# Three tiles move from one float32 product to split products with accumulating transfers, under a new instruction order

## The chip, the cores and the metric

The kernel runs on one core of a Trainium2 chip. The metric is the device time of one execution in microseconds, the median of several runs.

## What is computed

Four batches of eight heads run a gated linear recurrence over 768 steps of width 48; the result, 3072 tokens of width 384, goes through a feed-forward layer of width 2048 with a gate that is a clipped ramp.

```python
f = 1.0 / (1.0 + np.exp(-f_logit))
for t in range(S):
    state = f[:, :, t, :, None] * state + np.einsum('bhd,bhe->bhde', k[:, :, t], v[:, :, t])
    y[:, :, t] = np.einsum('bhd,bhde->bhe', q[:, :, t], state)
...
h = x @ w_in
relu6 = np.clip(h + 3.0, 0.0, 6.0)
g = h * relu6 / 6.0
return (g @ w_out)
```

## The kernel before

**Units and groups.** The recurrence is cut into 24 units, each one batch and one chunk of 128 steps. Four units (one chunk of all batches) make a group of 512 tokens, and there are six groups. On a unit i the steps are: `load`, `loadq`, `loadv` (transfers that SyncE issues), `gate` (sigmoid, ScalarE), `back` and `fwd` (scans, VectorE, L428 and L448), `kmul` and `qmul` (VectorE, L441 and L454), `rend` (two short VectorE instructions, L444 and L445), then on TensorE `tk` (transposes, L516), `kv` (L537), `att` (L497), `qs` (L571) and `av` (L587), with ScalarE's `ktok` (L523) between `tk` and `kv`, VectorE's `mask` (L504) between `att` and `av`, and `xh`, `xs`, `xl` that write the group's input rows.

**The feed-forward layer.** There are 16 slices f of the width 2048. For each group and slice, `mm1` multiplies into a PSUM bank, `relu` (ScalarE) and `g` (VectorE) form the gated value, and `mm2` adds to three PSUM banks. Numbers after these names count 16 per group, so `mm2.5` is slice 5 of group 0. Values are split into a high and a low float16 part: `gh` writes the high part on ScalarE (L683), `gl` the low part as a subtraction (L693), and `mm2` then needs nine float16 products (L709). For group 0 the slices 0 to 4 are done in halves (`mm1a`, `mm1b`, `mm2a`, `mm2b`) with float32 second products (L846), and slices 5 to 7 have `mm2x` (L720), three float32 products of 512 columns straight from the gated value. Groups 2 to 5 use a recombined form of the first product (`p1` to `p8`, L772).

**Weights.** Each slice's weights arrive as raw 64-bit numbers (`ld`, L284) and are turned to numbers by `z`, `cy` (ScalarE), `mid`, `dif`, `top` (VectorE, L301, L308, L312), then split: `high` on ScalarE (L317) and `low`, or its halves `lowi` (first product) and `lowo` (second product), by subtraction (L320).

**What sets the order.** `ORDER` is one list of steps; each step appends its instructions to its engine's queue, and every engine runs its queue in that order. So the list alone decides what stands behind what on PE, DVE, ACT, POOL and SP. `ON_POOL` names steps that GpSimd does in VectorE's place. `warm.n` (L1071) puts n blocks of 128 columns of products on zeros into TensorE's queue, whose result nobody reads. `hold` makes a step of a PSUM pair wait for the last `qs` there.

**The end.** The last group is written in two full thirds (`od.15`, `od.16` with 256 KB each) and two halves (`odh`), by ScalarE's queue. `flag0`, `finite`, `count` and `judge` gather a number that decides whether a slow general path follows.

## Time and profile before

| What | Value |
|---|---|
| median of 3 runs | 456.9 us (456.84 to 457.68) |
| the profiled execution's own time | 457.2 us |
| its span, first to last instruction | 455.5 us |
| TensorE busy | 448.7 us, 99% of the span |
| VectorE, ScalarE, GpSimd busy | 358.3, 231.2, 18.7 us |

The profiled execution spends 1.7 us outside its span and is 0.3 us longer than the median. A row of the chain of waits gives the start, the length and the engine and line of a piece of the work that ended last. A row of the timeline gives start, length, engine, line, operation, tiles, shapes and count, and in brackets the idle time before it with what ended it. Neighbouring instructions of an engine overlap by some 0.05 to 0.1 us in the timeline, and matmuls' ends are modelled.

### The profile page before, as it was taken

Reading aid. Unit: us, or ns where it says so; the run is one execution under the profiler, and the core shown is the slowest. Engines: PE = TensorE matmul, PEld = TensorE weight load, DVE = VectorE, ACT = ScalarE, POOL = GpSimd, SP = SyncE. Lnnn points to the kernel's source line nnn. Section 1 sums busy time; section 2 is a strip of 40 time slices with the busy share of each in tenths; the row PEclk is TensorE's granted clock in tenths of the full one; section 3 lists DMA queues with packets and bytes.
Section 4 is the critical chain, followed back from the end, with each engine's and each line's share of the span. In section 5 each row is a group of like instructions: output and inputs, shape, how many; then the busy total and the mean of one; then the engine's idle time right before and its main releaser. Section 6 shows DMA issues by size and latency. Waiting matters only on the chain.

```text
span 455.5 us, 12559 instructions
## 1 busy us (share of the span) xinstructions
PE 448.7 (99%) x5449; PEld 291.5 (64%) x5449; DVE 358.3 (79%) x643; ACT 231.2 (51%) x389; POOL 18.7 (4%) x31
## 2 busy tenths in 40 slices
PE   8899999999999999999999999999999999999996
PEld 4578755544455556686767676666676757677764
DVE  6999999879999999989986764888583676466562
ACT  3776777765454445554454265255263444442531
POOL 3000211231000000000000000000000000000000
PEclk9999999999999999999999999999999999999999
DMA  8679556550142512204202340040000010030002
GB/s 284 221 257 388 221 192 250 204 167 4 52 130 95 164 47 76 92 3 121 89 1 85 83 150 6 22 142 2 1 10 1 5 30 2 1 115 2 1 0 73
DMA packets 25531, 43.18 MB, mean 95 GB/s; under 512 B 2560, under 2 KB 17408, under 8 KB 25472
## 3 DMA queue, kind: packets, MB, share of 16 engines
q1 hardware_dynamic: 23872, 41.56, 27.1%
q8 instruction: 43, 0.70, 0.6%
q10 hardware_dynamic: 1600, 0.79, 0.6%
q14 instruction: 16, 0.13, 0.1%
HBM read 36.43 MB, written 4.72 MB: 90 GB/s over the span
## 4 chain that ended last, share of the span: by engine, by line
PE 96%; DVE 2%; ACT 1%; issue 0%; DVEq 0%; ACTq 0%
PE o L709 35%; PE pair L772 16%; PE single L772 9%; PE pair L664 7%; PE single L664 5%; PE pair L497 3%; PE o L846 3%; PE pair L587 3%; PE pair L571 3%; PE pair L537 2%; PE idle L1071 2%; PE o L720 2%; PE pair L516 2%; PE pair L862 1%; PE o_half L862 1%; PE single L828 1%
## 5 line engine op out<-in xcount | busy, mean ns | idle before, releaser
L709 PE MATMUL o<-gg,weight 128*128 128x512 f16 x744 | 173.4, 379 | 0.0
L709 PEld LDWEIGHTS <-weight 128*128 128x128 f16 x744 | 71.7, 98 | 73.8
L772 PEld LDWEIGHTS <-weight 128*128 128x128 f16 x672 | 65.1, 98 | 13.3 <-issue 0.2
L772 PE MATMUL pair<-xmem,wide 128*128 128x256 f16 x384 | 51.2, 273 | 0.0
L683 ACT ACTIVATE gg<-raws 128x512 f16<-128x512 f32 x64 | 38.4, 624 | 23.9 <-DVE raws L806 8.1
L772 PE MATMUL single<-xmem,weight 128*128 128x256 f16 x384 | 49.8, 273 | 0.2 <-DVE raws L806 0.2
L801 ACT ACTIVATE raws<-pair,half 128x512 f32<-128x512 f32 x32 | 21.5, 684 | 42.3 <-PE pair L772 33.3
L772 PEld LDWEIGHTS <-wide 128*128 128x128 f16 x384 | 36.9, 98 | 8.7 <-DVE single L787 0.6
L801 ACT ACTIVATE raws<-single,half 128x512 f32<-128x512 f32 x32 | 22.0, 687 | 39.8 <-PE single L772 32.2
L664 PEld LDWEIGHTS <-weight 128*128 128x128 f16 x243 | 23.1, 98 | 26.7 <-issue 0.3
L772 PE MATMUL pair<-xmem,weight 128*128 128x256 f16 x288 | 36.5, 273 | 0.0
L806 DVE SCALAR_TENSOR_TENSOR raws<-raws,single 128x512 f32<-128x512 f32 x32 | 21.8, 682 | 18.3 <-ACT raws L801 18.3
L693 DVE TENSOR_TENSOR gg<-raws,gg 128x512 f16<-128x512 f32 x48 | 31.9, 683 | 5.0 <-ACT gg L683 5.0
L664 PE MATMUL pair<-xmem,weight 128*128 128x512 f16 x144 | 33.2, 379 | 0.0
L806 DVE SCALAR_TENSOR_TENSOR raws<-raws,pair 128x512 f32<-128x512 f32 x32 | 21.5, 682 | 12.3 <-ACT raws L801 12.1
L787 DVE TENSOR_TENSOR pair<-pair,raws 128x512 f32<-128x512 f32 x16 | 11.2, 697 | 25.3 <-PE pair L772 17.1
L448 DVE TENSOR_TENSOR_SCAN suffix<-gates,rend 112x516 f32<-112x516 f32 x24 | 29.6, 1235 | 0.1
L428 DVE TENSOR_TENSOR_SCAN suffix<-gates,unit 112x516 f32<-112x516 f32 x23 | 28.0, 1223 | 0.1
L664 PE MATMUL single<-xmem,weight 128*128 128x512 f16 x99 | 23.2, 380 | 0.0
L674 ACT ACTIVATE tg<-pair,half 128x512 f32<-128x512 f32 x16 | 10.9, 686 | 19.5 <-PE pair L664 16.3
L683 ACT ACTIVATE gg<-tg 128x512 f16<-128x512 f32 x24 | 14.4, 626 | 9.0 <-DVE tg L678 5.2
L504 DVE TENSOR_TENSOR a<-pair,causal 128x512 f32<-128x512 f32 x24 | 16.3, 684 | 2.3 <-PE pair L497 1.3
(133 smaller groups left out, 639.5 us busy)
## 6 DMA issues: line engine op xcount, KB each, us to landing
qkf<-qk SPq DMA_DIRECT2D x24, 512.0 KB, 4.6
raws<-w SPq DMA_DIRECT2D x16, 768.0 KB, 5.7
gates<-fg SPq DMA_DIRECT2D x23, 258.5 KB, 3.6
v<-v SPq DMA_DIRECT2D x24, 200.0 KB, 3.7
outT<-os SPq DMA_DIRECT2D x11, 256.0 KB, 3.1
outT<-os SPq DMA_DIRECT2D x8, 128.0 KB, 1.9
wide<-wide SPq DMA_DIRECT2D x32, 24.0 KB, 2.0
outT<-os ACTq DMA_DIRECT2D x2, 256.0 KB, 4.1
```

The source lines that it names most:

```text
L428: nc.vector.tensor_tensor_scan(flat(sf)[:, ::-1], gt[:, 1:][:, ::-1], flat(unit)[:, ::-1], 0.0, op0=ALU.mult, op1=ALU.add,)
L448: nc.vector.tensor_tensor_scan(flat(sf), gt[:, :NP * (C + 1)], flat(rend), 0.0, op0=ALU.mult, op1=ALU.add,)
L497: nc.tensor.matmul(d["at"][HC * odd:HC * (odd + 1), e, 2 * n + c], t[rs, 1, n, c, odd], t[rs, 0, n, c, odd], start=not growing[at], stop=T ...
L504: nc.vector.tensor_tensor(d["a"].rearrange("r p e t -> r e p t"), d["at"], causal.unsqueeze(1).unsqueeze(1).broadcast_to([128, 2, NP, HC]) ...
L571: nc.tensor.matmul(d["y"][to:to + 64, odd, n, cs], before[rs, p], t[rs, 0, n, c, odd], start=alone and (odd, e) not in seen, stop=False, s ...
L664: nc.tensor.matmul(h, win[:, f, a, k * 128:(k + 1) * 128], g["xt"][:, k, :g["n"] // C, b], start=i == 0, stop=i == 3 * KT - 1,)
L683: nc.scalar.activation(d["gg"][:, 0], d["t"], AF.Copy)
L693: engine("gl", int(g["name"]) * NF + f).tensor_tensor(d["gg"][:, 1], d["t"], d["gg"][:, 0], op=ALU.subtract)
L709: nc.tensor.matmul(g["o"][m], wout[:, f, a, m * 128:(m + 1) * 128], g[f]["gg"][:, b], start=f == 0 and i == 0, stop=f == NF - 1 and i == 2 ...
L772: nc.tensor.matmul(to[:, n * 256:(n + 1) * 256], weights(q, n, a), g["wide"][:, :, block - 3, b], start=fresh and count == 1, stop=count = ...
L801: nc.scalar.activation(to, src, AF.Relu, bias=half, scale=RISE)
L806: nc.vector.scalar_tensor_tensor(to, to, TOP, src, op0=ALU.min, op1=ALU.mult)
```

## The change

1. The slices 5, 6 and 7 of group 0 no longer use three float32 products but nine float16 products as the others do. Their low parts are made without a subtraction: ScalarE writes the negated high part (`gn` for the gated value, `lno` for the weights), and GpSimd issues a transfer that adds the float32 value to it, from SBUF to SBUF (`gl.5` to `gl.7` and `lowo.5` to `lowo.7`, in the list `ON_DMA`). There are six such transfers, three `gn`, three `lno` and three more `gh`.
2. All of `ORDER` is another permutation. The blocks of `warm` are the same ten steps with 39 blocks, at other places. One `seed` (a product on zeros ahead of `count`) is gone.
3. Ahead of each `qs` a new `apart` puts a wait into TensorE's queue for the last `att`, `kv` or `av` of the same PSUM pair.
4. Of the four last transfers, three are issued by SyncE; the last one, of the second half, stays on ScalarE.

```diff
+ON_DMA = """
+gl.5 gl.6 gl.7 lowo.5 lowo.6 lowo.7
+""".split()
 ORDER = """
-load.0 loadh.0 gate.0 gateh.0 back.0 backh.0 loadq.0 loadv.0 rend.0 kmul.0 load.1 fwd.0 gate.1 back.1 warm.16 tk.0.3
...
+warm.16 load.0 loadh.0 gate.0 warm.4 warm.1 gateh.0 back.0 backh.0 rend.0 loadq.0 loadv.0 warm.1 warm.3 warm.3 load.1
...
+    def apart(at):
+
+        if touched[at] is not None:
+            after(nc.tensor.nop().ins, touched[at], mybir.DependencyClass.Sync)
+            touched[at] = None
+
+    def touch(at):
+        touched[at] = nc.cur_bb.bb.instructions[-1]
...
+    def conv_minus(f, half):
+        nc.scalar.activation(two(weight[:, f, 1])[:, half], both(f)[:, half], AF.Copy, scale=-1.0)
+
     def conv_low(op, f, half):
+        if f"{op}.{f}" in ON_DMA:
+            nc.gpsimd.dma_start(
+                out=two(weight[:, f, 1])[:, half], in_=both(f)[:, half], accum_op=ALU.add
+            )
+            return
...
         def qs():
             t = chunks[i]
             at, half = pair()
+            apart(at)
...
+    def gneg(g, f):
+        d = g[f]
+        nc.scalar.activation(d["gg"][:, 1], d["t"], AF.Copy, scale=-1.0)
+
     def glow(g, f):
         d = g[f]
+        if f"gl.{int(g['name']) * NF + f}" in ON_DMA:
+            nc.gpsimd.dma_start(out=d["gg"][:, 1], in_=d["t"], accum_op=ALU.add)
+            return
...
-            (nc.scalar if g is groups[-1] else nc.sync).dma_start(
+            (nc.scalar if g is groups[-1] and part == 1 else nc.sync).dma_start(
```

`touch(at)` is called at the end of `att`, `kv` and `av`.

TensorE's queue, from its first products to unit 0's `kv`, before (L1071 is `warm`, L516 `tk`, L537 the first of 48 products of `kv`):

```order
L1071 MATMUL idle<-blank 128x512 x4
L516 MATMUL pair_71<-ident,qkf_137 128x112 x4
L1071 MATMUL idle<-blank 128x512
L537 MATMUL pair_70<-v_139,ktok_156 64x48
L537 MATMUL pair_70<-v_139,ktok_156 48x48
```

The same place now (L1103 is `warm`, L538 `tk`, L559 `kv`):

```order
L1103 MATMUL idle<-blank 128x512 x5
L1103 MATMUL idle<-blank 128x128 x2
L1103 MATMUL idle<-blank 128x384 x2
L538 MATMUL pair_71<-ident,qkf_145 128x112 x4
L1103 MATMUL idle<-blank 128x128
L1103 MATMUL idle<-blank 128x512
L1103 MATMUL idle<-blank 128x128
L559 MATMUL pair_70<-v_147,ktok_165 64x48
L559 MATMUL pair_70<-v_147,ktok_165 48x48
```

Ahead of the first `tk` stand 28 blocks of `warm` in place of 16, between it and `kv` 6 in place of 4; fewer are left for later.

VectorE's queue between the low parts of the weight slices 0 and 1, before (L320 is `lowi`, L308 `dif`, L454 `qmul.3`, L312 `top`, L841 the gate `ga.0`, L504 `mask.3`):

```order
L320 TENSOR_TENSOR weight<-wide,weight 128x384
L308 TENSOR_TENSOR top_377<-top_377,raws 128x768
L454 TENSOR_TENSOR qkf_325<-qkf_325,suffix_77 112x512
L312 SCALAR_TENSOR_TENSOR wide<-top_377,wide 128x2x384
L841 SCALAR_TENSOR_TENSOR th_0_461<-th_0_461,single 128x256
L504 TENSOR_TENSOR a_488<-pair_71,causal 128x2x4x64
L320 TENSOR_TENSOR weight<-wide,weight 128x384
```

The same place now (L339 is `lowi`, L319 `dif.1` and `dif.2`, L312 `mid.2`, L526 `mask.3`, L323 `top`, L449 `back.4`, L873 `ga.0`):

```order
L339 TENSOR_TENSOR weight<-wide,weight 128x384
L319 TENSOR_TENSOR top_333<-top_333,raws 128x768
L312 TENSOR_SCALAR raws<-top_428 128x768
L526 TENSOR_TENSOR a_482<-pair_71,causal 128x2x4x64
L323 SCALAR_TENSOR_TENSOR wide<-top_333,wide 128x2x384
L449 SCALAR_TENSOR_TENSOR suffix_79<-gates_78,unit 112x516
L319 TENSOR_TENSOR top_428<-top_428,raws 128x768
L873 SCALAR_TENSOR_TENSOR th_0_523<-th_0_523,single 128x256
L339 TENSOR_TENSOR weight<-wide,weight 128x384
```

`mid.2`, `back.4` and `dif.2` now stand ahead of the second `lowi`, and `qmul.3` has moved ahead of the first; `back.2`, which stood behind `mask.0`, now stands ahead of it.

GpSimd's queue now, over the stretch with the six transfers (L462 is `kmul`, L339 `lowi`, L478 `decay`, L335 `lowo`, L717 and L725 `gl`):

```order
L335 DMA weight<-wide 128x384
L462 TENSOR_TENSOR qkf_951<-qkf_951,suffix_79 112x512
L717 DMA gg_5_890<-tg_5_887 128x512
L339 TENSOR_TENSOR weight<-wide,weight 128x384
L478 TENSOR_TENSOR decayed_108<-state_113,ends 112x4x48
L335 DMA weight<-wide 128x384 x2
L717 DMA gg_6_1078<-tg_6_1018 128x512
L717 DMA gg_7_1135<-tg_7_1063 128x512
L725 TENSOR_TENSOR gg_9_1230<-tg_9_1143,gg_9_1230 128x512
```

None of the DMA rows stood there before; `gl.6` stands behind two other transfers, and `gl.9` behind `gl.7`.

## Rows read from the trace of the kernel before

**Rows 1.** The page: busy time of each engine, share of the span, instructions.
```profile
PE 448.7 (99%) x5449; PEld 291.5 (64%) x5449; DVE 358.3 (79%) x643; ACT 231.2 (51%) x389; POOL 18.7 (4%) x31
```

**Rows 2.** Busy time by stretch: length, PE, PEld, DVE, ACT, POOL, clock, DMA.
```profile
12.00:24.00 12.00, 10.79 (x252) 7.04 (x241) 11.70 (x20) 8.74 (x16) 0.00 (x0) 1.00 0.63 220
24.00:36.00 12.00, 11.69 (x290) 9.66 (x290) 11.06 (x18) 10.38 (x19) 0.51 (x1) 1.00 0.68 254
...
240.00:264.00 24.00, 23.94 (x354) 15.70 (x352) 16.68 (x28) 9.08 (x15) 0.00 (x0) 1.00 0.33 98
264.00:288.00 24.00, 23.87 (x255) 16.79 (x255) 13.85 (x27) 13.04 (x27) 0.00 (x0) 1.00 0.19 56
```

**Rows 3.** The chain of waits over second products: start, length, engine, line, count.
```profile
58.72 2.77 PE o L720 x6
...
71.94 2.58 PE o L720 x6
...
82.34 1.94 PE o L709 x9
...
87.24 2.05 PE o L709 x9
```

**Rows 4.** The chain of waits at the start.
```profile
1.13 6.25 PE idle L1071 x8
7.37 0.39 PE pair L516 x4
7.76 0.87 PE idle L1071 x2
8.63 0.84 PE pair L537 x41
...
9.93 0.74 PE pair L497 x32
```

**Rows 5.** The timeline of VectorE from `mask.0` to `lowi.1`.
```profile
10.76 0.69 DVE L504 TENSOR_TENSOR a<-pair,causal 128x512 f32<-128x512 f32 x1 [1.28 <-PE pair L497]
...
13.24 1.23 DVE L428 TENSOR_TENSOR_SCAN suffix<-gates,unit 112x516 f32<-112x516 f32 x1
...
15.31 0.35 DVE L301 TENSOR_SCALAR raws<-top 128x768 int16<-128x768 int16 x1
...
16.86 0.53 DVE L308 TENSOR_TENSOR top<-top,raws 128x768 int16<-128x768 int16 x1
...
26.96 0.42 DVE L841 SCALAR_TENSOR_TENSOR th<-th,single 128x256 f32<-128x256 f32 x1 [0.76 <-ACT th L837]
...
27.98 0.55 DVE L320 TENSOR_TENSOR weight<-wide,weight 128x384 f16<-128x384 f32 x1
```

**Rows 6.** The timeline of TensorE: the second `mm1a`.
```profile
29.61 1.16 PE L828 MATMUL single<-xmem,weight 128*128 128x256 f16 x9
```

**Rows 7.** DMA issues: tiles, queue, count, KB each, median us from issue to landing.
```profile
raws<-w SPq DMA_DIRECT2D x16, 768.0 KB, 5.7
...
outT<-os SPq DMA_DIRECT2D x11, 256.0 KB, 3.1
...
wide<-wide SPq DMA_DIRECT2D x32, 24.0 KB, 2.0
```

**Rows 8.** The timeline: a SyncE issue, ScalarE's `z`, GpSimd's `gl.9`.
```profile
4.11 0.43 SPq L284 DMA_DIRECT2D raws<-w  x1
...
14.21 0.94 ACT L288 ACTIVATE wide<-raws 128x768 int32<-128x768 uint32 x1
...
81.11 1.18 POOL L693 TENSOR_TENSOR gg<-tg,gg 128x512 f16<-128x512 f32 x1 [7.33 <-ACT gg L683]
```

**Rows 9.** The chain of waits at the end: the `seed` ahead of `count`.
```profile
451.39 0.21 PE pair L809
```

**Rows 10.** The timeline of VectorE at the end: first of `flag0`, then `finite`.
```profile
449.42 0.24 DVE L959 TENSOR_REDUCE table<-ends 112x1 f32<-112x96 f32 x1
...
451.06 0.17 DVE L981 TENSOR_SCALAR sound<-sums 128x31 f32<-128x31 f32 x1
```

More of the change, by code (lines that the diff above doesn't have):

```diff
@@ L500, in att @@
                 )
+            touch(at)
         def mask():
@@ L993, in gla_moe @@
     MOE = {
-        "mm1": mm1, "relu": relu, "g": gate6, "gh": ghigh, "gl": glow, "mm2": mm2, "mm2x": mm2_whole,
+        "mm1": mm1, "relu": relu, "g": gate6, "gh": ghigh, "gl": glow, "gn": gneg, "mm2": mm2, "mm2x": mm2_whole,
         "mm2m0": lambda g, f: mm2(g, f, [0]), "mm2m1": lambda g, f: mm2(g, f, [1]),
```

191 lines of the change are left out of this document (97 added, 94 removed).

## The prediction

> **What bounds the kernel now.** I read the page's busy times first, then busy time by stretch, the chain of waits, and the timeline at the three places that the change touches. TensorE is busy for 448.7 us of 455.5, and no other engine comes near over the whole span [rows 1]. The reader should see that its 6.8 us of idle time are not spread: 1.2 us lie between 12 and 24 us, 0.3 between 24 and 36, and between 240 and 288 us it is 23.94 and 23.87 of 24 [rows 2]. So from some 30 us on the time is the sum of TensorE's products, and only three things can move it: fewer products, a later or earlier start of the dense stretch, and new waits. Part of the start's busy time is `warm`, which does nothing: eight passes take 6.25 us, and two later ones 0.87 [rows 4]. Over the start VectorE is the second bound, with 11.70 of 12 us and 11.06 of 12 busy [rows 2].
>
> **Second products of slices 5 to 7.** One tile's float32 products take 2.77 us the first time and 2.58 the last, and there are three tiles, the middle one like the last; nine float16 products take 1.94, or 2.05 where they follow small tiles [rows 3]. All of it is on the path. 2.77 + 2 x 2.58 - 3 x 1.94 = 2.1 us gained, 1.8 if each new set pays 2.05. I take 2.1.
>
> **Regrouping of small tiles.** `tk` apart, TensorE leaves its large products for a run of `att`, `kv`, `qs` and `av` 37 times after the start in the old order and 36 times in the new. Leaving such a run costs about 2.05 - 1.94 = 0.1 us [rows 3]. Gain 0.1.
>
> **The one wait of the dense stretch.** The windows around 264 us lack 0.06 + 0.13 = 0.2 us [rows 2]. The place does not exist in the new order; I take the 0.2 as gone, and put new waits under the rivals.
>
> **`warm` moved to the front.** The queue of TensorE has 28 blocks ahead of unit 0's `tk` where it had 16, and 6 between `tk` and `kv` where it had 4. A block costs 0.87 / 4 = 0.22 us once the clock is high [rows 4]. So `tk` moves from 7.37 to 7.37 + 12 x 0.22 = 10.0, ends 0.39 later, six blocks take 1.3, `kv` 0.84, `att` 0.74 [rows 4]: 13.3 us, and `mask.0`, which began at 10.76 [rows 5], begins at 13.3, 2.5 later. Nothing else can fill TensorE there, because every step behind waits for this unit. ScalarE's `gate.2` stands behind `ktok.0` and is late with it, so the time is not free for VectorE either, which in that gap has only `back.2` and `rend.1` to do.
>
> **VectorE from `mask.0` to `lowi.1`.** Before, this lasts from 10.76 to 28.53, 17.8 us, with one wait of 0.76 ahead of `ga.0` [rows 5]. The new order takes `back.2` out of the stretch (1.23) and puts `mid.2` (0.35), `back.4` (1.23, priced as `back.2`) and `dif.2` (0.53) in; with three more instructions ahead of `ga.0` its wait goes [rows 5]: -1.23 + 0.35 + 1.23 + 0.53 - 0.76 = +0.1. So `lowi.1` ends at 13.3 + 17.9 = 31.2, and the second `mm1a`, which waits for it and began at 29.61 [rows 6], begins 1.6 us later. At that point both orders have done the same steps on TensorE and neither has `warm` left, so the 1.6 is lost for good. The bounds: 0.4, if instructions overlap more closely than before, and 2.8, if ScalarE, which does `gate`, `z`, `cy` and `xh` in another order, holds VectorE up by 1.2, as long as one scan. I take +1.6, which follows from the nearest rows.
>
> **ScalarE's nine new instructions.** Three each of `gh`, `gn` and `lno`, at most 0.94 us each by the longest of its rows [rows 8], 8.5 us. ScalarE is busy for 51% of the span [rows 1], and TensorE has other products to do between a slice's `mm1` and its `mm2`: I take nothing. Uncovered, one of them would cost its 0.94. VectorE loses three `lowo` of 0.55 [rows 5], worth nothing while TensorE is the bound.
>
> **The accumulating transfers.** No row shows one. Landing: between 2.0 us (24 KB within SBUF) and 5.7 (768 KB), and 3.1 for a store of 256 KB, the nearest in size [rows 7]. Issue by GpSimd: between SyncE's 0.43 and the 1.18 of a GpSimd pass over the same data [rows 8]; I take 0.8. The tightest is `gl.6`. After `mm1.7` ScalarE does `relu.7`, `gh.6`, `gn.6`, `high.9` and `lno.6`, 3.9 us if they last some 0.8 each, then GpSimd issues three transfers, 2.4, and the last lands after 3.1: 9.4 us. TensorE meanwhile has `mm1.8`, `mm2.5`, `mm1.9` and `mm2.8`, 4 x 1.94 [rows 3], and four small steps of at most 0.74 [rows 4], some 10 us. I take no wait, by 0.6 us.
>
> **`apart`.** 18 waits in TensorE's queue. The product waited for lies 19 or more products ahead, so it should be done. Between 0 and 0.1 each (the restart price above), 2 us in all; I take 0.
>
> **The end.** The `seed` ahead of `count` costs 0.21 on the chain [rows 9] and goes. The closing waits name six more queues; no row prices that, I give the 0.2 back. The transfer that ends last stays with ScalarE, so those that SyncE takes gain nothing. `flag0` lasts from 449.42 to 451.06, 1.6 us [rows 10], and now stands ahead of `gl.93`; VectorE's eight passes of 0.69 [rows 5] ahead of it and `flag0` make 7.2 us, and TensorE has some 7.8 us of second products left then (seven thirds of 1.94, ten halves of those [rows 3]). Nothing taken, 0.5 in the range.
>
> **The sum**, against the profiled execution's 457.2 us: -2.1 - 0.1 - 0.2 + 1.6 - 0.2 + 0.2 = -0.8, 456.4. That execution is 0.3 above the median, so the median of the new kernel should be 456.1. About 0.9 us (0.2%) is what a measurement of this kernel can tell from no change, so the forecast itself lies at the edge between faster and the same.
>
> **Rivals.**
>
> The start is not later: VectorE and ScalarE make up for the blocks in front, because the new order has less waiting in the start than I count. Then -2.1 - 0.1 - 0.2 = -2.4 and 454.5. For it: between 24 and 36 us VectorE idles for 0.9 us [rows 2]. Against it: between 12 and 24 it idles for 0.3 only, so little can be made up. Chance 0.16.
>
> The transfers are late: with 1.18 per issue, 5.7 for the landing and 4.7 on ScalarE, `gl.6` lands 13.9 us after `mm1.7`, and `mm2.6` waits 3.9 us with all of TensorE's queue behind it. It decides from 10 us on; halfway 1.5 to 2, 457.6 to 458.1, slower or the same. For it: the margin is 0.6 us, and VectorE is busy nearly all the time there. The Trainium skill, SBUF — State Buffer, section "A bandwidth-pool intuition that's wrong", tells of a GpSimd-issued transfer that took 620 ns alone and 3100 beside a VectorE copy, as its descriptors wait for a port that VectorE holds; an estimate by that figure would put 2.5 us on each of the three transfers, and nothing in this trace shows it. Against it: the trace's GpSimd pass of 1.18 us ran at a time when VectorE was busy. Chance 0.18.
>
> TensorE's clock falls: between unit 0's `att` and the second `mm1a` there were 18 blocks of `warm`, now there are 5, and TensorE waits in between. The granted clock was 1.00 while it was busy for 10.79 of 12 us [rows 2]; with the blocks gone it is busy for perhaps 7 of 12. If it falls to the lower level (1.2 GHz of 2.4), the dense stretch begins at half rate until it rises again: at the start eight passes took 6.25 us and would take 4 x 0.87 = 3.5 at the high level [rows 4], 2.8 us lost. That gives 458.9, slower. The Trainium skill, TensorE: Matmul & The Clock Gate, Part 1, says that the throttled state is the default and activity releases it; the eight slow passes agree with that, and no row shows a fall within the kernel. Against it: single waits of the new start are about 1 us long. Chance 0.15.
>
> **How the numbers follow.** My forecast has 0.51, with a range of its own of 454.9 to 457.3 from the bounds of the start; about half of that is faster by more than 0.2%, half within. Faster: 0.25 + 0.16 = 0.41. Slower: 0.11 of the late transfers and 0.14 of the clock, 0.25. The same: 0.34. The range leaves out a tenth on each side: 454.2, a little below the second case with overlaps better still, and 458.6, between the late transfers and the clock.
>
> **What would show it.** Right: TensorE's `idle` rows in front end near 10 us, `mask.0` starts near 13.3, the second `mm1a` near 31.2, the rows of `mm2.5` to `mm2.7` are 1.9 to 2.1 us each, no idle time of TensorE between 36 and 445 us, and a total some 0.8 below. Wrong: idle time of TensorE ended by a transfer into `gg` or `weight` between 60 and 85 us (late transfers), the spacing of half-width products doubled after 25 us or a clock below 1.00 (clock), `mm1a.1` at 29.6 or earlier (the start), or a new wait further on that I have not named.

## The result: 1.3% slower

The changed kernel takes 463.5 us (median of 460.8 to 464.3), the one before 457.1: a ratio of 1.013, 95% interval 1.0101 to 1.0159. The prediction, 456.1 us with a range up to 458.6, was wrong in size and in sign. Single executions differ, in part by how long TensorE's clock was low: the one at a mean granted clock of 1.000 took 460.8 us, the four at 0.995 took 462.5 to 464.3, a spread that the clock does not account for.

The profiled execution took 462.45 us, its span is 460.7, 5.2 longer than before. First the page of the changed kernel: busy time of each engine, share of the span, instructions.

```profile
PE 448.1 (97%) x5454; PEld 291.9 (63%) x5457; DVE 363.4 (79%) x640; ACT 234.4 (51%) x398; POOL 30.0 (7%) x37
```

TensorE is busy 0.6 us less than in [rows 1], so its idle time, span less busy, went from 6.8 to 12.6. The span's +5.2 is +5.8 of idle time and -0.6 of work. Where the idle time lies, busy time by stretch tells (columns as in [rows 2], with GB/s last):

```profile
12.00:24.00 12.00, 10.21 (x345) 7.70 (x336) 11.43 (x21) 8.80 (x17) 0.00 (x0) 1.00 0.86 328
24.00:36.00 12.00, 10.66 (x222) 8.49 (x224) 11.60 (x22) 11.38 (x22) 3.44 (x2) 1.00 0.70 234
...
60.00:72.00 12.00, 10.58 (x140) 6.14 (x139) 11.96 (x17) 9.18 (x15) 2.65 (x4) 1.00 0.70 220
72.00:84.00 12.00, 12.00 (x176) 6.25 (x174) 11.90 (x20) 9.71 (x16) 6.73 (x6) 1.00 0.89 218
84.00:96.00 12.00, 10.04 (x130) 5.29 (x129) 8.63 (x13) 6.75 (x11) 2.04 (x2) 0.86 0.35 113
...
240.00:264.00 24.00, 24.00 (x293) 16.70 (x295) 19.19 (x33) 9.57 (x17) 0.00 (x0) 1.00 0.24 76
264.00:288.00 24.00, 24.00 (x297) 16.79 (x293) 16.09 (x29) 12.63 (x26) 0.00 (x0) 1.00 0.23 69
```

Between 60 and 96 us, where the three slices are computed, TensorE now idles for 1.4 + 2.0 us, and its clock is at the lower level (1.2 of 2.4 GHz) for part of the last stretch. VectorE has no free time left: 0.04 and 0.10 us idle in the two stretches from 60 to 84. Before, TensorE idled there for nothing and VectorE for 0.9 us in each:

```profile
60.00:72.00 12.00, 12.00 (x138) 6.36 (x137) 11.09 (x18) 8.64 (x14) 1.38 (x2) 1.00 0.69 263
72.00:84.00 12.00, 12.00 (x170) 6.12 (x169) 11.11 (x21) 9.55 (x14) 2.84 (x3) 1.00 0.65 231
```

From 110 to 445 us TensorE idles for 0.2 us in either kernel. TensorE's longest waits behind 30 us (us in total, times, longest), and four rows of its timeline:

```profile
PE o L741 <- DMA gg<-tg: 2.0, 1, 2.0
PE pair L518 <- DVE qkf L475: 0.9, 1, 0.9
PE pair L860 <- DMA xmem<-xmem: 0.6, 1, 0.6
PE pair L595 <- DVE xmem L647: 0.5, 1, 0.5
```

```profile
30.07 1.14 PE L860 MATMUL single<-xmem,weight 128*128 128x256 f16 x9
...
63.37 0.46 PE L595 MATMUL pair<-qkf,decayed 48*64 48x64 f32 x16 [0.51 <-DVE xmem L647]
64.97 0.69 PE L518 MATMUL pair<-qkf 48*64 48x64 f32 x32 [0.91 <-DVE qkf L475]
...
87.03 0.81 PE L741 MATMUL o<-gg,weight 128*128 128x512 f16 x3 [1.96 <-DMA gg<-tg]
```

The longest wait, 1.96 us ahead of 87.03, is for the transfer `gl.7`; behind it the granted clock is low from 87.85 to 91.27, and products take twice as long for those 3.41 us, some 1.7 us more. The two smaller waits, 0.51 and 0.91, are for VectorE. VectorE's and GpSimd's timelines show what held it:

```profile
57.32 1.23 DVE L449 TENSOR_TENSOR_SCAN suffix<-gates,unit 112x516 f32<-112x516 f32 x1
...
59.84 2.90 DVE L469 TENSOR_TENSOR_SCAN suffix<-gates,rend 112x516 f32<-112x516 f32 x1
```

```profile
59.84 0.85 POOL L717 DMA_DIRECT2D gg<-tg  x1
...
60.46 1.18 POOL L339 TENSOR_TENSOR weight<-wide,weight 128x384 f16<-128x384 f32 x1
```

The scan `fwd.6` (59.84) takes 2.90 us where the scan ahead of it takes 1.23; during it GpSimd issues `gl.5` and makes the low part `lowi.7`.

To follow the loss I call **lag** the difference of the times at which the two kernels have done the same useful TensorE work (products at their usual length, `warm` left out). It is an estimate from the two timelines, good to about 1 us, because the two orders do different products at a given time: some 0.4 us at 30 us, 1.2 to 1.7 from 38 to 53, between 3.3 and 4.3 from 66 to 85, and from 90 us on 7 to 8. The saved products are 2.5 us of that scale, so some 5 remain. The steps at 60 to 66 and 85 to 94 us are the two places shown above.

### The profile page after: what moved, and what is told of

Same layout as the page of the kernel before. It is cut to its first block, busy times and chain, and to the rows that moved or that the text cites. A ratio compares the mean times of both kernels' runs of the same rounds, so it can differ in the third digit from the quotient of the medians.

```text
span 460.7 us, 12588 instructions
## 1 busy us (share of the span) xinstructions
PE 448.1 (97%) x5454; PEld 291.9 (63%) x5457; DVE 363.4 (79%) x640; ACT 234.4 (51%) x398; POOL 30.0 (7%) x37
## 4 chain that ended last, share of the span: by engine, by line
PE 84%; DVE 6%; ACT 3%; DMA 3%; issue 2%; SPq 0%
PE o L741 34%; PE pair L804 16%; PE single L804 9%; PE pair L689 6%; PE single L689 3%; PE pair L518 2%; PE pair L611 2%; PE pair L595 2%; PE idle L1103 2%; PE pair L559 2%; DMA gg<-tg 2%; PE pair L538 1%; PE o_half L894 1%; PE pair L894 1%; DVE wide L323 1%
## 5 line engine op out<-in xcount | busy, mean ns | idle before, releaser
L741 PE MATMUL o<-gg,weight 128*128 128x512 f16 x771 | 178.3, 379 | 2.0 <-DMA gg<-tg 2.0
L741 PEld LDWEIGHTS <-weight 128*128 128x128 f16 x771 | 74.6, 98 | 80.2 <-issue 2.2
L804 PEld LDWEIGHTS <-weight 128*128 128x128 f16 x672 | 65.0, 98 | 12.1
L689 PEld LDWEIGHTS <-weight 128*128 128x128 f16 x243 | 23.3, 99 | 28.4 <-issue 1.3
L725 DVE TENSOR_TENSOR gg<-raws,gg 128x512 f16<-128x512 f32 x48 | 32.0, 683 | 0.7 <-ACT gg L708 0.6
L469 DVE TENSOR_TENSOR_SCAN suffix<-gates,rend 112x516 f32<-112x516 f32 x24 | 31.1, 1296 | 0.3
L449 DVE TENSOR_TENSOR_SCAN suffix<-gates,unit 112x516 f32<-112x516 f32 x23 | 28.6, 1243 | 2.2 <-ACT gates L443 2.1
L819 DVE TENSOR_TENSOR pair<-pair,raws 128x512 f32<-128x512 f32 x16 | 11.2, 698 | 23.2 <-PE pair L804 12.3
L708 ACT ACTIVATE gg<-tg 128x512 f16<-128x512 f32 x27 | 16.5, 623 | 7.3 <-PE o L741 4.5
L323 DVE SCALAR_TENSOR_TENSOR wide<-top,wide 128x768 int16<-128x768 int16 x16 | 17.3, 1080 | 0.0
L545 ACT ACTIVATE ktok<-pair 128x448 f32<-128x448 f32 (+1 forms) x21 | 10.5, 505 | 13.0 <-PE pair L538 13.0
```

Of the source, the lines that this page charges most:

```text
L323: nc.vector.scalar_tensor_tensor(upper, two(conv[f]["y"]), 8.0, upper, op0=ALU.mult, op1=ALU.add)
L449: nc.vector.tensor_tensor_scan(flat(sf)[:, ::-1], gt[:, 1:][:, ::-1], flat(unit)[:, ::-1], 0.0, op0=ALU.mult, op1=ALU.add,)
L469: nc.vector.tensor_tensor_scan(flat(sf), gt[:, :NP * (C + 1)], flat(rend), 0.0, op0=ALU.mult, op1=ALU.add,)
L545: nc.scalar.activation(d["ktok"][:, ns], d["tk"][:, ns], AF.Copy)
L689: nc.tensor.matmul(h, win[:, f, a, k * 128:(k + 1) * 128], g["xt"][:, k, :g["n"] // C, b], start=i == 0, stop=i == 3 * KT - 1,)
L708: nc.scalar.activation(d["gg"][:, 0], d["t"], AF.Copy)
```

## The experiments

Eighteen kernels were run. In the texts quoted, A and B are the two theories that the run tells apart. Edits of the order are shown as steps of `ORDER` taken out (-) and put in (+). Times are medians, with the ratio to the kernel before.

### The wait for `gl.7`, alone

```diff
 mask.7
-mm2.7
 ld.13 kmul.8 ... top.13 mm1.12.1
+mm2.7
 av.7
```

> The changed kernel with one step moved on TensorE: the nine second products of slice 7 (mm2.7) stand behind mm1.12 instead of in front of tk.8, some 6 us later; nothing else moves. In the changed kernel the transfer gl.7 lands at 86.98 us, 8.1 us after its issue, TensorE stands from 85.06 to 87.03 for it, and the granted clock is at its lower level from 87.85 to 91.27 (the lag behind the kernel before grows there from about 3.9 to 7.5 us). Theory A (the late landing of gl.7 is the cause of both): the 1.96 us of idle time are gone, the clock stays 1.00, and the total falls by 2.0 + 1.7 = 3.7 us, from 463.5 to about 459.8. Theory B (TensorE is behind VectorE there, and the transfer is only what was waited for last): another wait of 1 us or more appears between 80 and 96 us and the total falls by under 2 us. Theory C (the clock falls for what TensorE missed between 60 and 68 us): the wait goes, the lower clock stays, and the total falls by 2.0.

463.0 us, 1.0137 (1.011 to 1.0163). In the profiled execution the wait is gone and so is the fall of the clock, but only 0.5 us of the median, less than the executions differ (461.5 to 464.4). Two of the others had a mean clock of 0.992 and 0.996, so the clock still falls in some. In the next window TensorE and ScalarE wait for something else (the waits of each, 80 to 100 us and 80 to 86 us):

```profile
PE pair L690 <- DVE weight L340: 2.3, 1, 2.3
```

```profile
ACT wide L300 <- DMA raws<-w: 2.0, 1, 2.0
```

Load 13 lands at 84.10, although slice 13 is used before slice 14, whose load stands ahead of it and lands at 81.12; ScalarE's conversion waits 2.0 for it, then VectorE's low part is late and TensorE waits 2.3. B holds: the next limit stood right behind the removed one.

### GpSimd's low part beside VectorE's scan

```diff
 ON_POOL: ... kmul.7 decay.7
-lowi.7
 kmul.8 gl.9 ...
```

> The changed kernel with lowi.7 (0.92 to 1.18 us on GpSimd) given to VectorE (0.55 us). In the changed kernel VectorE's scan fwd.6 lasts from 59.84 to 62.73, 2.90 us where this scan lasts 1.23 elsewhere, and TensorE then stands for 0.51 us before qs and 0.91 before att. During that scan GpSimd issues the transfer gl.5 (59.84 to 60.69) and does lowi.7 (60.46 to 61.63). Theory A (VectorE's passes over two SBUF operands and GpSimd's passes hold each other up): the scan falls to at most 1.23 + 0.85 = 2.1 us, the two waits of TensorE, 1.4 us together, shrink by 0.25 to 1.1 us (the scan saves 0.8 to 1.65, lowi.7 costs VectorE 0.55), and so does the total of 463.5. Theory B (issuing the accumulating transfer is what stops the scan): the scan still lasts 2.4 us or more, and with the 0.55 on VectorE the waits are as long as before or longer.

462.6 us, 1.0129 (1.0104 to 1.0153). A holds: with the issue of `gl.5` still beside it and only GpSimd's pass gone, the scan is back at its usual length (timelines of VectorE and GpSimd):

```profile
59.36 1.22 DVE L469 TENSOR_TENSOR_SCAN suffix<-gates,rend 112x516 f32<-112x516 f32 x1
```

```profile
59.35 0.85 POOL L717 DMA_DIRECT2D gg<-tg  x1
```

The waits of 0.51 and 0.91 are gone. TensorE is then earlier and waits longer for `gl.7`, 3.2 us instead of 2.0: what one place gives back the next takes. The median's 0.9 us is within the spread of the executions; the timelines are what shows the cause.

### The wait for `gl.7` once more, with load 13 ahead of load 14

```diff
 g.9 loadv.8
+ld.13
 ld.14 ... mask.7
-mm2.7 ld.13
 kmul.8 ... mm1.12.1
+mm2.7
```

> The changed kernel with mm2.7 behind mm1.12, as in the run before, and the load of slice 13 ahead of that of slice 14 on SyncE. With mm2.7 behind mm1.12 alone TensorE stood for 2.34 us before 88.68 for the low part of slice 12 or 13, VectorE for 1.7 us before 85.91 and ScalarE for 2.0 before 84.18, for the load of slice 13, which landed at 84.10 while that of slice 14, not needed yet, landed at 81.12. Theory A (the load is the next limit behind gl.7): ScalarE starts slice 13 near 81.5, the wait of TensorE shrinks from 2.3 to under 0.5, and the time falls to about 461. Theory B (VectorE is behind as a whole): slice 13 starts earlier but TensorE waits as long for VectorE, in this place or the next, and the time stays within 0.5 of 463.0.

460.1 us, 1.0057 (1.004 to 1.0074), and the wait of 2.3 is 0.5. A holds. All four executions had a mean clock of 1.000.

With `lowi.7` on VectorE as well:

```diff
 ON_POOL: ... kmul.7 decay.7
-lowi.7
 kmul.8 gl.9 ...
```

> As the run before it in this list (mm2.7 behind mm1.12, load 13 ahead of load 14), and lowi.7 on VectorE, which by itself gave fwd.6 its normal 1.23 us back and brought VectorE ahead by 1.3 to 1.7 us up to 83 us, a lead that the wait for gl.7 then used up. Theory A (VectorE's time is the bound between 48 and 84 us): the lead lasts, and this kernel is 1.3 us or more below the run without lowi.7 moved, near 459.5. Theory B (from 84 us on other chains decide): no more than 0.4 below it.

458.9 us, 1.0034 (1.002 to 1.0048), 1.2 less than without it, near A. From here on *the three moves* are `mm2.7` behind `mm1.12`, load 13 ahead of load 14, and `lowi.7` on VectorE. Together they give 4.6 us back. `mm2.7` alone and `lowi.7` alone gave 0.5 and 0.9; load 13 was not moved alone. Part of the 4.6 is the clock, which is now at 0.998 or above in every execution: against the one execution of the changed kernel at 1.000, 460.8, it is 1.9.

### The premise: are the second products on the path?

The kernel before, with the three steps `mm2x` left out, so that slices 5 to 7 are missing from the result:

```diff
 g.5
-mm2x.5
 cy.7 ... low.8
-mm2x.6
 mm1.8.0 ... rend.8
-mm2x.7
 ld.11
```

> The kernel before with the float32 second products of slices 5 to 7 (mm2x.5, mm2x.6, mm2x.7) left out altogether, with nothing in their place; every other step keeps its place. It takes 2.77 + 2 x 2.58 = 7.9 us of products off TensorE. Theory A (as in the prediction, all of it is on the path): the time falls by 7.9, from 457.2 to 449.3, and TensorE gets no new wait. Theory B (these products fill time in which the weights of the next slice are not converted yet: in the kernel before the low parts of slices 6, 7, 8, 9 and 10 are ready at 60.88, 65.71, 69.87, 76.06 and 79.77 us, and the products that use them come 0.9 to 2 us later): TensorE waits for weights of slices 6 to 10, most of the 7.9 us comes back as idle time between 58 and 90 us, and the time falls by 1 to 3 us only; if the clock falls behind these waits, by less still.

458.7 us, 1.003 (1.0018 to 1.0041): taking 7.9 us of products away makes the kernel no faster. B holds in its mechanism, and the gain that it still expected, 1 to 3 us, is not there: six of the seven executions had a mean clock of 0.996. The profiled one is the seventh, at 1.000, with 456.8 us, 0.4 less than the profiled execution before. In it TensorE idles for 6.7 us between 48 and 84. TensorE's waits of 1 us and more between 56 and 100 us, and its busy time from 60 to 84 (first column behind the length):

```profile
PE pair L497 <- DVE xmem L622: 2.5, 1, 2.5
PE single L664 <- DVE tg L678: 1.6, 1, 1.6
PE pair L664 <- ACT weight L317: 1.5, 1, 1.5
PE single L664 <- ACT weight L317: 1.0, 1, 1.0
```

```profile
60.00:72.00 12.00, 7.88 (x123) 3.93 (x123) 11.73 (x18) 9.15 (x14) 1.46 (x2) 1.00 0.65 255
72.00:84.00 12.00, 10.10 (x168) 5.79 (x168) 11.78 (x21) 9.40 (x14) 2.84 (x3) 1.00 0.69 242
```

TensorE idles 6.0 us in 24 and waits for VectorE, busy for 11.73 and 11.78, and for ScalarE. So between 60 and 84 us the kernel before had two engines nearly level, and its float32 products filled time in which TensorE would have waited. The trace of before held this, in rows that I had not read: the low parts of slices 7 to 10 (timeline of VectorE and, for slice 7, GpSimd) and the first products that use slices 7, 8 and 9 (timeline of TensorE).

```profile
64.79 0.92 POOL L320 TENSOR_TENSOR weight<-wide,weight 128x384 f16<-128x384 f32 x1
68.91 0.96 DVE L320 TENSOR_TENSOR weight<-wide,weight 128x768 f16<-128x768 f32 x1
75.11 0.95 DVE L320 TENSOR_TENSOR weight<-wide,weight 128x768 f16<-128x768 f32 x1
```

```profile
65.31 2.10 PE L664 MATMUL single<-xmem,weight 128*128 128x512 f16 x9
69.83 2.10 PE L664 MATMUL pair<-xmem,weight 128*128 128x512 f16 x9
76.34 2.12 PE L664 MATMUL single<-xmem,weight 128*128 128x512 f16 x9
```

Slice 8's low part ends at 69.87, about where its products begin; slice 9's ends at 76.06 for a start at 76.34. There was hardly any slack for TensorE to move into.

### Split and order apart

The split alone, in the order of before, each new step put where its inputs are ready:

```diff
 high.5
+lno.5
 qs.4.2 ... g.5
-mm2x.5
+gh.5 gn.5 gl.5
 cy.7 ... mm1.7.4
+mm2.5
 relu.7
```

and so for slices 6 and 7.

> The code of the changed kernel with the order of the kernel before: slices 5 to 7 are split by accumulating transfers as in the change (lno, gn, gh, lowo and gl stand right behind the steps that they need), mm2.5 stands behind mm1.7, mm2.6 behind mm1.9, mm2.7 behind mm1.11; all other steps stand as before. Theory A (the split itself gains the 2.1 us of the prediction, and the loss is the order's): no idle time of TensorE ended by a transfer, the clock stays 1.00, and the time is 457.1 - 2.1 = 455.0 us. Theory B (the transfers cost wherever they are, because GpSimd and VectorE hold each other up while they are issued and TensorE waits for VectorE): VectorE's instructions between 55 and 85 us are longer by 1 us or more together, TensorE is idle there for 1 us or more, and the time is 456.5 to 459.

466.9 us, 1.0225 (1.0192 to 1.0259), more than either theory expected. Its waits, 2.2 us for `high.6` (which stood behind the new `gh.5` and `gn.5` on ScalarE) and 2.3 for `lowi.7` (behind the issue of `gl.6` on GpSimd), come from my placing, so a second version puts `gh`, `gn` and `gl` behind the parts of the weights (slice 5 is shown):

```diff
 g.5
-gh.5 gn.5 gl.5
 cy.7 ... high.6
+gh.5 gn.5
 lno.6 ... lowi.6
+gl.5
 lowo.6
```

> The split in the order of the kernel before once more, with its new steps placed so that they hold up nothing that I can see: gh.5 and gn.5 behind high.6 on ScalarE, gh.6 and gn.6 behind high.8, gh.7 and gn.7 behind high.9, gl.6 behind lowi.7 on GpSimd; mm2.5 behind mm1.7, mm2.6 behind mm1.9, mm2.7 behind mm1.11. In the first try mm1.6 waited 2.16 us for high.6, behind gh.5 and gn.5, and mm1.7 2.28 us for lowi.7, behind the issue of gl.6. Theory A (the split costs only where its steps stand in the way of others): 457.2 - 2.1 = 455.1. Theory B (the weights of slices 6 to 10 are ready just in time, so that what TensorE saves comes back as waits): about as without any second products of these slices, waits of 1 to 2.5 us at mm1.6, mm1.7, mm1.8 and att.7, and since the products are still to be done behind them the time is 459 to 464.

464.2 us, 1.0154 (1.0136 to 1.0172), about B's upper end. B holds: the waits change places and do not go (TensorE, 56 to 100 us), and behind the longest of them the clock is low from 73.2 to 76.6.

```profile
PE pair L520 <- DVE xmem L649: 2.3, 1, 2.3
PE single L691 <- ACT weight L330: 1.4, 1, 1.4
PE single L691 <- DVE tg L705: 0.9, 1, 0.9
```

Now the new order without the split, with `mm2x` at the places of `mm2.5` to `mm2.7` and `lowo.5` to `lowo.7` back on VectorE, later:

```diff
 qmul.7
-mm2.5
+mm2x.5
 low.9 ...
-lno.5 lowo.5 gh.5 gn.5 gl.5
```

> The changed kernel's order without the split: slices 5 to 7 have their float32 second products (mm2x) at the places where mm2.5 to mm2.7 stand, and the steps gh, gn, gl, lno of the three slices and their accumulating transfers are gone; lowo.5 to lowo.7 are done on VectorE later, where the kernel before has them. TensorE has 2.1 us more of products than in the changed kernel. Theory A (up to 90 us VectorE and ScalarE set the pace, and the products of slices 5 to 7 fill time in which TensorE would wait): the 2.1 cost nothing, the wait of 1.96 for gl.7 and the lower clock behind it are gone, and the time is 459.5 to 461. Theory B (the split gains its 2.1 us also here and the loss has other reasons): the time is 463.5 + 2.1 - 3.7 = 461.9 or more.

459.9 us, 1.0048 (1.0031 to 1.0065), with no wait of TensorE between 38 and 105 us. The time is A's. The four corners:

| | no split | split |
|---|---|---|
| order of before | 457.1 | 464.2 |
| order of after | 459.9 | 463.5 |

The split costs 3.6 us in the order made for it and 7.1 in the other; the order alone costs 2.8. The corner 457.1 is the kernel before itself; the other three also have `apart` and the other queues of the last transfers, whose share no run shows by itself. And with the three moves the split stands at 458.9, 1.0 below the order alone, which has none of them: whether the split gains or costs in the new order once the same moves are made on both sides was not run.

### What held `gl.7`

In the changed kernel the six transfers land after these times (DMA issues: count, KB each, median us to landing; then the range for the three `gl`):

```profile
gg<-tg POOLq DMA_DIRECT2D x3, 128.0 KB, 4.7
weight<-wide POOLq DMA_DIRECT2D x3, 96.0 KB, 4.0
```

```profile
DMA to landing us min/median/max: 3.6/4.7/8.1
```

The 8.1 is `gl.7`. Three things could hold it: GpSimd's passes, VectorE's passes, or the two weight loads issued just ahead. All three runs below start from the version with the three moves. First GpSimd's `kmul.8` and `gl.9` go to VectorE:

```diff
 ON_POOL: ... decay.7
-lowi.7 kmul.8 gl.9
 decay.8 ...
```

> As the run before it in this list, and gl.9 and kmul.8 on VectorE too, so that GpSimd has no pass behind its issue of gl.7. In the changed kernel gl.7 was issued from 78.90 to 79.77, its first packets moved at 83.62, after GpSimd's passes gl.9 and kmul.8 (79.64 to 82.94) and VectorE's passes over two SBUF operands beside them (79.67 to 80.70 and 81.93 to 83.36), and it landed at 86.98. Theory A (the passes that GpSimd does behind the issue hold the descriptors back): packets move within 1.5 us of the issue and gl.7 lands 3.5 to 5 us after it. Theory B (VectorE's passes hold them back): as VectorE now does 1.4 us more of such passes there, gl.7 still lands 6 us or more after its issue. For the time: VectorE's dif.12 and mid.12 fall from 1.42 and 0.66 us to 0.55 and 0.35, it gets 0.68 + 0.68 more, so the time stays within 0.5 of the run without this edit.

458.9 us, 1.0039 (1.0027 to 1.0051). The first packet of `gl.7` moves at 81.66, 3.5 us after its issue ended, as before. GpSimd's passes alone are not the cause. Then VectorE's:

```diff
 cy.12
-mid.12 dif.12
 mm1.10.1 ... g.10 mask.7
+mid.12 dif.12
 kmul.8
```

> The changed kernel with mm2.7 behind mm1.12, load 13 ahead of load 14 and lowi.7 on VectorE, and with VectorE's passes mid.12 and dif.12 (operands in SBUF only) behind g.10 and mask.7 (which read PSUM), so that behind top.11 VectorE has some 2 us of passes that read PSUM. In all runs so far the first packets of gl.7 moved 0 to 0.3 us after the end of dif.12, 3.5 to 4.4 us after GpSimd had finished the issue, with GpSimd's passes behind the issue (81.96, 82.24) and without them (81.66). Theory A (VectorE's passes over two SBUF operands keep GpSimd from writing the descriptors): the packets move within 0.6 us of the end of top.11, near 80.5, and gl.7 lands near 84, 2.5 to 3 us earlier than the 86.4 and 87.0 of the runs without this move. Theory B (the transfer is slow by itself, 8 to 9 us when GpSimd has issued three others shortly before): it lands at 86 or later.

458.6 us (one execution). VectorE has no pass with two operands in SBUF from 79.3 to 82.2, and the first packet still moves only at 81.91. Not VectorE's alone either. Last, load 14 into another buffer and behind `mask.7`, so that it is issued at 82 us instead of 76.4:

```diff
 loadv.8
-ld.14
+ld.13
 low.10 ... mask.7
-mm2.7 ld.13
+ld.14
 kmul.8 ... mm1.12.1
+mm2.7
...
-        raw = raws[:, RAW * turn_of("raw", 3):][:, :RAW]
+        n = turn_of("raw", 3)
+        raw = raws[:, RAW * {14: 0, 15: 2}.get(f, n):][:, :RAW]
```

> The changed kernel with mm2.7 behind mm1.12, load 13 ahead of load 14 and lowi.7 on VectorE (458.9 us), and load 14 (768 KB) into the buffer that slice 12 leaves instead of that of slice 11, so that it is issued near 82 us instead of 76.4; load 15 takes the other buffer. In every run of the changed order gl.7's first packets moved 3.5 to 4.1 us after the end of its issue, without GpSimd's passes behind it (81.66) and without VectorE's (81.91) as with both (82.24); at that time two weight loads were under way (landing at 80.2 and 84.2). Where none was, the first packets of such a transfer moved 0.57 to 0.69 us after the issue, and with one 0.6 to 2.7. Theory A (gl.7 waits behind the two loads): with one load under way its packets move within 2.7 us, before 80.8, and it lands before 84. Theory B (passes of VectorE or GpSimd, whichever comes, hold it): first packets near 82 and landing near 86 to 87 as before. For the time: mm2.7 does not wait in either case, so 458.9 within 0.6, if load 14 is not late for slice 14 (start near 89.8).

458.8 us, 1.0039 (1.0027 to 1.0051). The first packet moves 0.74 us after the issue, and `gl.7` lands after 4.0. A holds: one load ahead of it, issued at 75.3, does not hold it, two did. The DMA queues from 78.2 to 82.2 us (packets, MB, share of the engines), first of the version with the three moves, which has both loads ahead, then of this one:

```profile
q1 hardware_dynamic: 181, 0.87, 79.5%
```

```profile
q0 software_dynamic: 144, 0.13, 28.5%
q1 hardware_dynamic: 62, 0.28, 17.0%
```

With both loads there is no row for q0, GpSimd's queue, at all. The landing of `gl.7` is explained; the time does not move, since `mm2.7` stood far enough behind by then.

### The start

Blocks of `warm` back at their old places in the changed kernel:

```diff
-warm.16
 load.0 loadh.0 gate.0
-warm.4 warm.1
 gateh.0 ... kmul.0
+warm.16
 tk.0.3 ... xh.0 fwd.2
+warm.3
 att.1.0
```

and the others likewise.

> The changed kernel with the blocks of warm put back to the places that they had in the kernel before (16 ahead of unit 0's tk, 4 ahead of its kv, the rest ahead of the same steps as there); every other step keeps its place. Theory A (the start is 1.5 us later because of the blocks in front, as the prediction had it): mask.0 starts near 10.8 instead of 13.25, the lag at 45 us falls from 1.6 to about 0, and the total falls by 1.5, from 463.5 to 462.0. Theory B (the start is bound by VectorE and the loads in the new order): mask.0 starts earlier but the second mm1a still starts near 30.1, and the total stays within 0.5 of 463.5.

462.1 us, 1.0104 (1.0087 to 1.0121). `tk` of unit 0 starts at 7.59, near the 7.37 of [rows 4], but `mask.0` only at 12.82, because VectorE is at the scan `back.2` from 10.42 to 12.63, 2.2 us beside GpSimd's `kmul.1`. The second `mm1a` starts at 31.21, later than with the blocks in front. Inconclusive: the median went A's way, by less than the executions differ, the trace against A. The scan was moved next (on top of the three moves):

```diff
 ld.0
-back.2
 loadq.2 rend.1 carry0.0 mask.0 fwd.1
+back.2
 rend.2
```

> The changed kernel with mm2.7 behind mm1.12, load 13 ahead of load 14 and lowi.7 on VectorE (458.9 us), and with VectorE's scan back.2 behind fwd.1 instead of ahead of mask.0. The blocks of warm stay in front. Theory A (the blocks set the start): mask.0 starts at 13.2 as before, since att.0 ends at 12.9, and the time stays within 0.4 of 458.9. Theory B (VectorE's order sets it): mask.0 starts earlier by 0.4 or more, the lag at 45 us falls below 1.0, and so does the time by as much.

461.4 us, 1.0077 (1.0053 to 1.01), 2.5 slower than without, against both theories: `mask.0` starts at 12.84, the clock is low from 18.8 to 32.4, and the second `mm1a` starts at 34.0. And both together, with `tk.8` one place later:

```diff
 low.11
-tk.8.1 ktok.8
 high.12 ... mm1.11.0
+tk.8.1 ktok.8
 gh.10
```

> As the run before it in this list, and the blocks of warm at the places of the kernel before, and tk.8 behind mm1.11 (TensorE waited 0.65 us for tk.8 while mm1.11 was ready). With the blocks alone put back, mask.0 started at 12.82, since back.2, lengthened from 1.23 to 2.21 us beside GpSimd's kmul.1, stood ahead of it. Theory A (the two together make the start late): mask.0 starts before 11.5, the lag at 45 us falls from 1.5 to 0.3 or less, and with 0.6 for tk.8 the time is 458.9 - 1.2 - 0.6 = 457.1 or a little below, no slower than the kernel before. Theory B (the start is bound by the loads and VectorE's sum of work): the lag at 45 us stays above 1 and the time above 458.

460.4 us, 1.0059 (1.004 to 1.0078). `mask.0` starts at 10.90, as early as before, and yet the second `mm1a` at 32.64, as the clock is low from 11.2 to 18.0. With `tk.8` moved, `qs` waits 1.1 us for a `mask`, at 85.2. Neither theory fits the time. But the three runs together answer what makes `mask.0` late: the blocks back (first line, its own run) or the scan back (second) leave it near 12.8, both back (third) bring it to 10.90. Either one holds it.

```profile
12.82 0.66 DVE L527 TENSOR_TENSOR a<-pair,causal 128x512 f32<-128x512 f32 x1
12.84 0.69 DVE L527 TENSOR_TENSOR a<-pair,causal 128x512 f32<-128x512 f32 x1 [1.42 <-ACT middle L574]
10.90 0.69 DVE L527 TENSOR_TENSOR a<-pair,causal 128x512 f32<-128x512 f32 x1 [0.89 <-ACT middle L574]
```

The last of this kind leaves 12 blocks in front of `tk` out, on top of the version with load 14 later:

```diff
 gate.0
-warm.4 warm.1
 gateh.0 ... loadv.0
-warm.1 warm.3 warm.3
 load.1
```

> As ld14_later (458.8 us), without the 12 blocks of warm that the change added ahead of unit 0's tk; the 16 first and the 11 behind tk stay. Over the runs so far tk.0 of the changed start began 3.0 to 4.7 us after the clock had risen, between 8.65 and 10.16, and mask.0 3.6 later, between 12.27 and 13.79. Theory A (the 12 blocks are what makes the start late): tk.0 begins near 7.3 and mask.0 near 11, the second mm1a before 29.5 (30.5 in ld14_later, 29.61 in the kernel before), and the time falls by 1.0 to 1.5, to 457.3 to 457.8, level with the kernel before. Theory B (the blocks keep the clock up in a start that waits for VectorE): the clock falls to its lower level between 10 and 30 us, as in the two runs with moved blocks or a moved scan, and the time is 459 or more. Theory C (VectorE catches up in either case): mask.0 is earlier, the second mm1a within 0.5 of 30.5, and the time within 0.6 of 458.8.

460.8 us, 1.0064 (1.0046 to 1.0083), against 458.8 with them. `tk` comes 2.4 us earlier (6.97 against 9.39), `mask.0` 0.3 (12.67 against 13.01), and then the clock falls, here in its columns of the stretches, 0.67 and 0.76:

```profile
12.00:24.00 12.00, 9.66 (x259) 7.71 (x259) 11.00 (x20) 6.90 (x13) 0.00 (x0) 0.67 0.86 336
24.00:36.00 12.00, 11.73 (x236) 9.51 (x230) 10.50 (x19) 11.26 (x22) 2.88 (x2) 0.76 0.63 209
```

B holds. `back.2` lasts 2.2 us here too, right ahead of `mask.0`, so the blocks alone are not what makes the start late; and without them the clock falls. (The one execution of the seven with a mean clock of 0.998 took 458.3, as with the blocks.) Three more runs put the order of before up to the second `mm1a` in front of the order of after, first by itself:

```diff
-warm.16 load.0 loadh.0 gate.0 warm.4 warm.1 gateh.0 ...
+load.0 loadh.0 gate.0 gateh.0 back.0 backh.0 loadq.0 ... qs.3.2 av.3 xh.3 mm1a.1.4
 ld.3 load.5 cy.2 z.2 ...
```

> The order of the kernel before up to the second mm1a, and from there the order of the changed kernel (steps already done left out). The start of the changed kernel had a lag of 1.4 to 1.7 us behind the kernel before from 38 us on. Putting the blocks back alone did not take it away (lag 1.9 to 2.2), nor did moving back.2 (the clock fell in those starts). Theory A (the start's lag is the whole new order's there, and passes on to the end): the lag at 47 us is 0.3 or less and the time 463.5 - 1.5 = 462.0. Theory B (what the start loses is caught up anyway, since a later chain decides): the lag at 47 us falls but is back at 3.9 or more at 75 us, and the time stays within 0.5 of 463.5.

467.4 us, 1.024 (1.0194 to 1.0286). The seam makes a wait of 3.9 us (`mm2a` for VectorE's `ga`, behind other steps there), so neither theory is tested and the run tells nothing of the start. With the three moves (the edits shown for them above), and then without the split:

> As the run before it in this list, with the three moves that brought the changed kernel from 463.5 to 458.9: mm2.7 behind mm1.12, load 13 ahead of load 14, lowi.7 on VectorE. Theory A (the gains add up): 458.9 - 1.5 = 457.4, level with the kernel before. Theory B (VectorE's sum of work up to 90 us decides, not where the start stands): 458.4 or more, with waits of TensorE for VectorE between 50 and 90 us.

462.8 us, 1.0131 (1.0109 to 1.0153). 4.6 us less, as much as the three moves gave before. The wait of 3.9 is still there.

```diff
-mm2.5
+mm2x.5
...
-lno.5 lowo.5 gh.5 gn.5 gl.5
```

> The start of the kernel before and from the second mm1a on the changed kernel's order, without the split: slices 5 to 7 with float32 second products, no accumulating transfers, lowo.5 to lowo.7 later on VectorE; load 13 ahead of load 14 and lowi.7 on VectorE. Its TensorE has 2.1 us more of products than old_start_fixes. Theory A (the split's 2.1 us gain nothing in either order): the time is that of old_start_fixes within 0.6, or below it. Theory B (once the start, the loads and gl.7 are mended the split does gain): it is 1.5 or more above old_start_fixes.

464.9 us, 1.0169 (1.0143 to 1.0195), 2.1 us slower than with the split. B holds. It is the one pair of runs that has the moves on both sides, and in it the split gains what was predicted. A reason that would fit the rest, not shown by itself: behind a stall of 3.9 us the weights are ahead of TensorE, so TensorE is the bound and the shorter products count. Whether the moves would be enough without the stall is open.

## Why the prediction was wrong, step by step

Two steps failed: that what is saved on TensorE is saved in time, and that nothing new would make TensorE wait.

**Second products on the path (-2.1): the work fell, the premise failed.** The products came out as costed: the row of `mm2.5` is 2.1 us, and TensorE is busy 0.6 us less although some 1.7 went to the lower clock, so its work fell by some 2.3. "All of it is on the path" was the error. I read 23.9 busy of 24 us as a bound. The run without `mm2x` shows that in the order of before 7.9 us of products were worth 0.4 in its fastest execution and nothing in the median: TensorE and VectorE were nearly level, and TensorE had its weights just in time. What the split saved there went into waits. In the new order it is less plain. Without the split TensorE has no wait there from 38 to 105 us; as changed, the two waits below cost more than the split saves; and where both sides have the three moves, behind the old start, the 2.1 is gained.

**No wait for the transfers: failed, in place and size, and the dearest.** I took `gl.6` for the tightest and 5.7 us for the longest landing. It was `gl.7`, with 8.1, behind two loads of 768 KB. The issue was put at 0.8 and took 0.85 and more. The rival "transfers late" named the kind of wait, not its reason. The run that takes VectorE's passes away leaves the first packet where it was, and the one that moves a load ends the delay. The Trainium skill, SBUF — State Buffer, section "A bandwidth-pool intuition that's wrong", which I cited beside that rival, would have made a port held by VectorE the reason; it was not what held this transfer. The wait taken at nothing cost 1.96 and, with the low clock behind it, some 1.7 more, but removing it alone gave 0.5: load 13 was next.

**ScalarE's nine instructions at nothing: failed in the old order.** Ahead of `high.6` they made TensorE wait 2.2 us. In the new order no wait of TensorE is put down to them.

**Not named at all: GpSimd's passes beside VectorE's.** TensorE's two waits for VectorE between 60 and 66 us, 1.42 together, go when `lowi.7` leaves GpSimd. GpSimd's busy time rose from 18.7 to 30.0 us. In the changed kernel up to 84 us, VectorE's passes beside one of GpSimd's are 3.7 us longer in all than their usual length (an estimate, each pass against the median of its kind), in the one before 0.3. VectorE had 0.9 us of idle time in each of the two stretches from 60 to 84 to give.

**The start (+1.6): half right.** `mask.0` was predicted for 13.3 and came at 13.25. The second `mm1a` was predicted for 31.2 and came at 30.07, so 0.5 of lag in place of 1.6. Another 1 us came by 38 us, with a wait of 0.6 for a transfer into `xmem`. The blocks of `warm`, on which I put the whole delay, are one of two reasons for `mask.0`: `back.2`, now ahead of it, is the other, and either one alone holds it until 12.8 (2.2 us for `back.2` beside GpSimd's `kmul.1` when the blocks are away).

**The clock: a rival that came, in another place.** I put it into the start. In the changed kernel the clock held there and fell behind the wait for `gl.7`. In three variants of the start it did fall there, for 6.8 to 13.7 us, and in the new order without the split for 3.4.

**Right:** `apart` (0.2 us of idle time from 110 to 445 us, as before), the wait at 264 us gone (24.00 of 24 in both windows), and the end, where the last transfer's issue stands 3.62 us from the end of the span, 3.66 before.

**The sum.** By the two profiles TensorE's idle time is longer by 1.3 us up to 36 us, 0.6 from there to 60, 1.4 from 60 to 84, 2.2 from 84 to 110 and 0.2 behind 445; the low clock costs some 1.7 and the work is some 2.3 less: 5.1 of the span's 5.2. The forecast had 1.6 for the start and 2.1 for the work, near what came. It had nothing for the waits from 60 to 110 us and the clock behind them, 5.3 together. The three moves, which act there, give 4.6 back in the median. **Open** is the rest, the 1.8 us by which the best variants (458.6 to 458.9) are slower than before. In the one with load 14 later TensorE's waits from 36 us on are 1.2 us in all, and in the two stretches from 12 to 36 us (columns as above) it idles for 2.4 + 1.6 us, against 1.2 + 0.3 in [rows 2]:

```profile
12.00:24.00 12.00, 9.65 (x320) 7.28 (x318) 11.41 (x21) 8.51 (x17) 0.00 (x0) 1.00 0.88 337
24.00:36.00 12.00, 10.41 (x223) 8.37 (x221) 11.46 (x21) 11.81 (x22) 2.72 (x2) 1.00 0.63 221
```

So most of it lies in the start and some in those waits, while TensorE is busy for 2.5 us less than before over the whole span. My changes in the start each brought a low clock or a seam, and did not show which step costs it. No version beat the kernel before.

## What to carry to other kernels

An engine that is busy for 12 us of 12 need not be the only bound: before counting removed work as gained, read how long ahead of their use its inputs are ready, and, if it can be done, run once with that work left out. When two engines are level, look at what the change adds to the second one. Look at what is queued on the DMA engines ahead of a small transfer: here the same 128 KB landed after 4.0 or after 9.8 us.

## What the runs showed of the hardware

**GpSimd's passes and VectorE's lengthen each other**, here where VectorE's operands all lie in SBUF. The scan went from 1.23 to 2.90 us beside a GpSimd pass of 1.18 (and the issue of a transfer, which by itself left it at 1.22), and GpSimd's `gl.9` from 1.18 to 2.04; the passes that read PSUM, as `mask`, kept their 0.68. The Trainium skill, SBUF — State Buffer, section "SBUF: two separate sides", calls the shared ports an exclusive lock held for a whole instruction, also against a VectorE pass with two inputs in SBUF; the trace agrees that the one holds up the other, but not on the rest: the two passes in a row would be 1.23 + 1.18 = 2.4 us, the scan took 2.9, and it was the one that had begun first and ended last. Here the measurement decides.

**A transfer issued by GpSimd can stand behind large loads.** At best its first packet moved 0.57 to 0.74 us after the end of the issue and it landed 3 to 4 us after the issue's start (`lowo.5` landed only after 5.9 to 8.0 in the new order, with its first packet after 0.57); behind two loads of 768 KB the first packet took 3.5 to 4.1 us and the landing 8.1 to 9.8. In the changed kernel the queues from 79.8 to 83.6 us show one row:

```profile
q1 hardware_dynamic: 284, 1.07, 92.5%
```

The Trainium skill, DMA: Bandwidth & Descriptors, section "SWDGE vs HWDGE vs iDMA", has each DMA engine take turns among its queues. Here no packet of GpSimd's queue moved for 3.8 us while SyncE's did, so in this case the measurement decides; whether its descriptors stood ready in that time no trace shows.

**A wait can cost twice.** Behind the wait of 1.96 us TensorE ran at the lower level for 3.41 us; so it did behind the wait of 3.2 with `lowi.7` on VectorE and behind those of 3.9 with the old start, and the split in the old order, first version, has two such stretches of 3.4 us, at 61 and 71 us. It doesn't follow each time: in the profiled executions the wait of 2.3 us with `mm2.7` moved back and that of 2.5 without `mm2x` show no fall.
